# A compact second-stage table, 64-row tiles in the second inverse and a new order, in a two-layer long-convolution and MLP kernel

## The chip, the cores and the metric

The kernel runs on one core of a Trainium2 chip. Its engines are TensorE (PE in the profile; PEld is its weight load), VectorE (DVE), ScalarE (ACT), GpSimd (POOL) and SyncE (SP, which here only issues transfers). Each works through its own list of instructions in order and waits on semaphores for the others. The metric is device time in microseconds; less is better.

## The reference

Two layers follow each other twice, on x with 2048 rows of 512 channels (bfloat16), A being a gated long convolution over the rows and B a multilayer perceptron:

```python
x = A_q
x = x + _A_ref(_layernorm(x), A_k, A_v, A_shift_k, A_ssm_k, A_ssm_D)
x = x + _B_ref(_layernorm(x), B_w1, B_b1, B_w2, B_b2)
x = x + _A_ref(_layernorm(x), A_k, A_v, A_shift_k, A_ssm_k, A_ssm_D)
x = x + _B_ref(_layernorm(x), B_w1, B_b1, B_w2, B_b2)

def _A_ref(q, k, v, shift_k, ssm_k, ssm_D):
    kv = (causal 4-tap filter of k with shift_k) * v        # per channel
    y  = irfft(rfft(kv padded to 4096) * rfft(ssm_k padded to 4096))[:2048]
    return q * (y + kv * ssm_D)

def _B_ref(x, w1, b1, w2, b2):                              # 512 -> 1376 -> 512
    return gelu(_layernorm(x) @ w1 + b1) @ w2 + b2
```

The convolution's result y does not depend on x: it is computed once and serves both layers.

## The kernel before, in words

**The convolution.** The rows are taken in two halves of 1024, and the transform of length 2048 is done by matmuls in steps. For the filter h (`ssm_k`): `ht0` turns the loaded channels by PE transposes (L536), `h1_0` is the first stage (function `stage1`, L553, 128 matmuls of 64 weight columns), and `h2_0` the second stage (`stage2`, L565). A stage-two matmul has a 128x128 weight tile from the table `S2` and a moving operand of 64 columns. `S2` is in fact block-like: for each of the 128 frequencies, its 128 rows are the pairs (part, position, d) with d of 0 to 7, and row d only meets the column of the same d, so seven eighths of the table are zeros. The table of before is stored and loaded with its zeros, 16384 columns in 16 loads of 256 KB (L459). Results of `h2_0` are swapped between even and odd partitions by transfers in SBUF (`swap`, L449) to get real and imaginary parts beside each other.

For the data: `fir0` to `fir3` turn k (L585), run the 4-tap filter as matmuls (L610, 64-row tiles) and multiply by v (L616, VectorE); `x1_0` and `x2_0` are the two stages; products with the filter's transform (L464, VectorE) follow; `i1_0` and `i2_0` are the two steps of the inverse (`inverse1`, L665; `inverse2`, L683). The second half has the same steps with the suffix 1 (`h1_1`, `h2_1`, `p2`, `fir4` to `fir7` by L638 on 32-row tiles, `x1_1`, `x2_1`, `sum`, `i1_1`, `i2_1`). Its `i1_1` needs every product and sum of `x2_1`.

`inverse1` makes eight tiles of two PSUM banks each. For each of eight 128-column groups it adds two matmuls, weights 128x128 from the products p and q, moving operand 128 columns of the table `U`; one eviction of 1024 columns follows for each tile (L469 on ScalarE, L470 on VectorE).

**The layers.** Rows are worked in blocks of 128 to 512: `q` (statistics L797/L798, GpSimd's inverse root L804, a normalization L822 on ScalarE or L823 on VectorE), `y` (times y, add), `z` (the second normalization, then a turn on PE L874 or by a transfer L866), `m1` (L886, four matmuls for each of eleven tiles, Gelu on ScalarE L891) and `m2` (L920, eleven matmuls, added by VectorE L924). The last block's `m2` is cut in column pieces (L909, L913).

**The order.** The program first records all operations (`Prog.op`) with the memory they read and write. Then it takes them in an order written out as a list of numbers, `SEQ`. `ENGS` says for each operation with a choice which engine does it (a ScalarE, v VectorE, p GpSimd), and `BANKS` gives each PSUM tile its first bank. Each engine's list is that order restricted to it; waits are derived from the recorded dependences. Loads and other transfers that SyncE issues are in the same order, so a transfer that waits for data holds all that stand behind it.

```python
for i in range(16):
    tload(t_s2, 128 * 128, i * 1024, R_S2 + i * 1024, 1024)
tload(t_sm, row, 464, R_U, 256)
```

Of the kernel before, what the change touches and what calls it, by code (L numbers as in the profile page):

```python
# [36 lines left out]
class Prog:  # L37
# [62 lines left out]
            "avva")  # L100
    BANKS = ("02220326464004602026041320002442462264542202240064064646402046462667062260046446220462640604660406064226644472"
             "44450442172316353547502206314500451400554567076567013226140174645320543403764701436154766316307007062272260403"
             "71655156407602371631706316706615043246755274432051240747516203416017010")

    def __init__(self, nc):
        self.nc = nc
# [282 lines left out]
def bass_interleave_layers__ssm_conv_h3__mixer_channel_mlp__prompt_kernel(  # L389
# [3 lines left out]
    NS = 352  # L393
# [567 lines left out]
```

## Time and profile before

| | |
|---|---|
| timed runs, median (lowest to highest) | 239.39 us (238.99 to 239.71), 3 runs |
| the profiled execution, first to last instruction | 238.6 us; the profile has no other time for it |
| mean granted clock of TensorE | 0.993 |
| TensorE busy | 226.9 us, 95% |
| VectorE busy | 178.1 us, 75% |
| ScalarE busy | 159.6 us, 67% |
| GpSimd busy | 55.3 us, 23% |
| moved by the transfers | 26.75 MB |

A row of the profile names the engine, the line of the source, the operation, the tiles written and read ("ar" is the one SBUF buffer, "ps" PSUM, "sm" a small float32 buffer) and their shape. Since one helper line records many operations, line 464 stands for all tensor-tensor operations, 469 and 470 for all evictions, and 449 for most transfers. Matmul rows overlap: their own length is latency, and the pace is the distance of starts, which the chain of waits shows. In the chain each row is a start, a length and what ran.

### The profile page before, as it was taken

Reading aid. Unit: us, or ns where it says so; the run is one execution under the profiler, and the core shown is the slowest. Engines: PE = TensorE matmul, PEld = TensorE weight load, DVE = VectorE, ACT = ScalarE, POOL = GpSimd, SP = SyncE. Lnnn points to the kernel's source line nnn. Section 1 sums busy time; section 2 is a strip of 40 time slices with the busy share of each in tenths; the row PEclk is TensorE's granted clock in tenths of the full one; section 3 lists DMA queues with packets and bytes.
Section 4 is the critical chain, followed back from the end, with each engine's and each line's share of the span. In section 5 each row is a group of like instructions: output and inputs, shape, how many; then the busy total and the mean of one; then the engine's idle time right before and its main releaser. Section 6 shows DMA issues by size and latency. Waiting matters only on the chain.

```text
span 238.6 us, 6251 instructions
## 1 busy us (share of the span) xinstructions
PE 226.9 (95%) x2615; PEld 152.3 (64%) x2637; DVE 178.1 (75%) x358; ACT 159.6 (67%) x255; POOL 55.3 (23%) x120
## 2 busy tenths in 40 slices
PE   6998698899999999999999999999999999999995
PEld 3897588885968588667769675644445444444454
DVE  0579869999999999999999999593579469404013
ACT  2586879999996899999768786359036606831630
POOL 2421030104623506446004522303020210200000
PEclk9999979999999999999999999999999999999999
DMA  6999767989946660053100304200300050132202
GB/s 173 350 393 388 272 181 186 257 267 194 163 87 197 153 140 3 1 69 103 54 0 15 80 0 83 49 3 12 78 0 3 18 157 0 25 66 91 84 0 91
DMA packets 41112, 26.75 MB, mean 112 GB/s; under 512 B 23702, under 2 KB 33788, under 8 KB 41084
## 3 DMA queue, kind: packets, MB, share of 16 engines
q1 hardware_dynamic: 40786, 26.20, 40.5%
q8 instruction: 21, 0.34, 0.6%
q10 hardware_dynamic: 298, 0.16, 0.3%
q14 instruction: 7, 0.06, 0.1%
HBM read 15.07 MB, written 2.10 MB: 72 GB/s over the span
## 4 chain that ended last, share of the span: by engine, by line
PE 83%; DVE 6%; DMA 4%; ACT 3%; issue 2%; POOL 1%; SPq 1%; POOLq 0%
PE ps L886 32%; PE ps L920 31%; PE ps L665 6%; PE ps L553 5%; PE ps L565 3%; ACT ar L469 3%; DMA ar<-in_A_ssm_k_dram 2%; DVE ar L464 2%; DMA ar<-ar 2%; DVE ar L616 1%; PE ps L683 1%; PE ps L909 1%; PE ps L638 1%; PE ps L610 1%; DVE ar L470 1%
## 5 line engine op out<-in xcount | busy, mean ns | idle before, releaser
L891 ACT ACTIVATE ar<-ps,sm 128x256 bf16<-128x256 f32 (+4 forms) x143 | 65.4, 525 | 41.0 <-PE ps L886 39.5
L469 ACT ACTIVATE ar<-ps 128x1024 bf16<-128x1024 f32 (+3 forms) x77 | 71.3, 1005 | 16.4 <-PE ps L553 6.4
L886 PE MATMUL ps<-ar 128*128 128x256 bf16 (+4 forms) x568 | 81.5, 297 | 0.3
L920 PE MATMUL ps<-ar 128*128 128x512 bf16 (+1 forms) x324 | 77.2, 379 | 1.1 <-issue 0.3
L886 PEld LDWEIGHTS ps<-ar 128*128 128x128 bf16 (+1 forms) x572 | 52.8, 100 | 28.1 <-ACT ar L891 0.4
L464 DVE TENSOR_TENSOR ar<-ar 128x512 bf16<-128x512 bf16 (+3 forms) x105 | 62.7, 637 | 0.9 <-ACT ar L469 0.4
L920 PEld LDWEIGHTS ps<-ar 128*128 128x128 bf16 (+1 forms) x341 | 32.4, 98 | 33.4 <-ACT ar L891 0.2
L924 DVE TENSOR_TENSOR ar<-ar,ps 128x512 bf16<-128x512 bf16 x31 | 20.7, 678 | 33.2 <-PE ps L920 33.0
L797 DVE BATCH_NORM_STATS2 sm<-ar 128x6 f32<-128x512 bf16 x64 | 42.9, 683 | 0.5
L822 ACT ACTIVATE ar<-ar,sm 128x512 bf16<-128x512 bf16 x34 | 26.4, 811 | 9.5 <-DVE sm L809 8.3
L804 POOL TENSOR_TENSOR sm<-sm 128x2 f32<-128x2 f32 (+2 forms) x26 | 23.6, 909 | 23.8 <-DVE sm L802 22.0
L802 POOL TENSOR_SCALAR sm<-sm 128x2 f32<-128x2 f32 (+2 forms) x21 | 6.4, 304 | 97.3 <-DVE sm L798 97.1
L553 PE MATMUL ps<-ar 128*64 128x128 bf16 x512 | 18.6, 227 | 3.1 <-issue 1.4
L565 PEld LDWEIGHTS ps<-ar 128*128 128x128 bf16 x512 | 18.4, 102 | 3.4 <-ACT ar L469 1.0
L565 PE MATMUL ps<-ar 128*128 128x64 bf16 x512 | 19.6, 199 | 0.5 <-ACT ar L469 0.4
L553 PEld LDWEIGHTS ps<-ar 128*64 128x64 bf16 x512 | 15.7, 114 | 6.1 <-issue 2.6
L812 POOL TENSOR_SCALAR sm<-sm 128x1 f32<-128x1 f32 x43 | 16.1, 390 | 2.0
L470 DVE CAST ar<-ps 128x1024 bf16<-128x1024 f32 x11 | 13.3, 1222 | 4.3 <-PE ps L565 2.8
L665 PE MATMUL ps<-ar 128*128 128x128 bf16 x256 | 15.0, 219 | 0.5 <-DVE ar L464 0.4
L665 PEld LDWEIGHTS ps<-ar 128*128 128x128 bf16 x256 | 14.7, 113 | 1.2 <-DVE ar L464 0.6
L823 DVE TENSOR_SCALAR ar<-ar,sm 128x512 bf16<-128x512 bf16 x30 | 11.8, 410 | 3.4 <-POOL sm L812 3.1
L470 DVE COPY ar<-ps 128x1024 bf16<-128x1024 bf16 (+1 forms) x9 | 5.5, 632 | 8.0 <-PE ps L516 5.3
(41 smaller groups left out, 94.3 us busy)
## 6 DMA issues: line engine op xcount, KB each, us to landing
ar<-tab_s SPq DMA_DIRECT2D x16, 256.0 KB, 9.0
ar<-ar SPq DMA_DIRECT2D x16, 256.0 KB, 3.7
ar<-in_A_ssm_k_dram SPq DMA_DIRECT2D x8, 256.0 KB, 6.8
ar<-in_A_q_dram SPq DMA_DIRECT2D x8, 256.0 KB, 4.7
ar<-in_A_v_dram SPq DMA_DIRECT2D x8, 256.0 KB, 6.1
out_dram<-ar SPq DMA_DIRECT2D x7, 256.0 KB, 2.5
ar<-in_B_w_dram SPq DMA_DIRECT2D x4, 344.0 KB, 4.8
ar<-in_B_w_dram SPq DMA_DIRECT2D x5, 256.0 KB, 4.0
```

The lines of the kernel that those rows point to most:

```text
L464: return P.op(eng, lambda e: e.tensor_tensor(o, a, b, op), dur, reads=[a, b] + list(more), writes=[o])
L469: return e.activation(dst, src(), AF.Copy)
L470: return e.tensor_copy(dst, src())
L553: r = e.matmul(Q(tl, 64 * ri, 64, i * 128, [1, 128]), w, m, start=True, stop=True)
L565: r = e.matmul(Q(tl, 0, 128, i // 8 * 512 + i % 8 * 4, [32, 16], [1, 4]), w, m, start=True, stop=True)
L665: r = e.matmul(Q(tl, 0, 128, i * 128, [1, 128]), w, m, start=n == 0, stop=n == 1)
L797: P.op(DVE, lambda e, sj=sj, x=x: e.bn_stats(sj, x), 600.0, reads=[x], writes=[sj])
L804: P.op(POOL, lambda e: e.tensor_tensor(r, v, hf, ALU.pow), 420.0 + 149.0 * n, reads=[v, hf], writes=[r])
L822: return e.activation(o, x, AF.Identity, bias=u, scale=r)
L886: r = e.matmul(Q(tl, 0, rows, 0, [1, w]), a, m, start=dk == 0, stop=dk == 3)
L891: P.op(ACT, lambda e, dst=dst, tl=tl, rows=rows, bias=bias, w=w: e.activation(dst, Q(tl, 0, rows, 0, [1, w]), AF.Gelu_apprx_tanh, bias=bia ...
L920: r = e.matmul(Q(tl, 0, 128, 0, [1, 512]), ins[fc][0], ins[fc][1], start=fc == 0, stop=fc == 10)
```

## The change

Four things change.

1. The second-stage table is stored without its zeros, 2048 columns, and loaded in two pieces of 256 KB into the place where `w1` goes later (`R_C = R_W1`). Eight columns of 0 and 1 are added to the small table (`sg`), copied once to the float32 buffer (`M_MK`). Sixteen operations tagged `spread` build the dense table: for each half h and each d, the compact half (1024 columns) is multiplied by mask column d, which is 1 in the partitions of that d and 0 elsewhere, and written to 64 runs of 16 columns. Twelve are on VectorE (`tensor_scalar`), four on ScalarE (`activation` with Copy and a scale).
2. The order of the table's columns, and with it of the partitions behind stage two, puts d with the even values first; the table `U` is turned to match.
3. The second half's `inverse1` (`split`) uses 64-row tiles: for each of the 128 former matmuls two with 64 rows of weights, one for the upper and one for the lower 64 partitions, each with 64 moving columns (a strided view of `U`) into its own PSUM bank; 256 matmuls. The first half's stays as it was.
4. `SEQ`, `ENGS` and `BANKS` are new lists. Among other things the loads are reordered: the first are h, q, h, h, h, table, q, table, then four of k and, with one of q among them, four of v (before: h, h, h, four of k, h, q, four of v, h, and the sixteen table pieces among others).

```diff
 class Prog:
-    SEQ = (33, 34, 6, 214, 1, 44, 0,
...
+    SEQ = (
...
     c, s = np.cos(th), np.sin(th)
-    S2 = np.zeros((2, 8, 8, 128, 2, 8, 8))
-    for d in range(8):
-        S2[0, :, d, :, 0, :, d] = c
-        S2[1, :, d, :, 0, :, d] = s
-        S2[0, :, d, :, 1, :, d] = -s
-        S2[1, :, d, :, 1, :, d] = c
-    S2 = S2.transpose(0, 1, 2, 3, 5, 6, 4).reshape(128, 128 * 128)
+    S2 = np.zeros((2, 8, 8, 128, 8, 2))
+    S2[0, :, :, :, :, 0] = c[:, None]
+    S2[1, :, :, :, :, 0] = s[:, None]
+    S2[0, :, :, :, :, 1] = -s[:, None]
+    S2[1, :, :, :, :, 1] = c[:, None]
+    S2 = S2.reshape(128, 2048)
...
-    U = U.transpose(1, 2, 0, 3, 4, 5, 6).reshape(128, 256)
+    U = U[:, :, [0, 2, 4, 6, 1, 3, 5, 7]].transpose(2, 1, 0, 3, 4, 5, 6).reshape(128, 256)
...
+    sg[:, 8:] = np.arange(128)[:, None] % 8 == np.array([0, 2, 4, 6, 1, 3, 5, 7])
...
+    for i in range(2):
+        tload(t_s2, 2048, i * 1024, R_C + i * 1024, 1024)
...
-    for i in range(16):
-        tload(t_s2, 128 * 128, i * 1024, R_S2 + i * 1024, 1024)
+    mk, src = M(0, 128, M_MK, [1, 8]), A(0, 128, R_SG + 8, [1, 8])
+    P.op((DVE, POOL), lambda e, mk=mk, src=src: e.tensor_copy(mk, src), {DVE: 65.0, POOL: 190.0}, reads=[src], writes=[mk])
+    for h in range(2):
+        for d in range(8):
+            o, c, m = A(0, 128, R_S2 + 8192 * h + 16 * d, [128, 64], [1, 16]), A(0, 128, R_C + 1024 * h, [16, 64], [1, 16]), M(0, 128, M_MK + d, [1, 1])
+            def f(e, o=o, c=c, m=m):
+                if e is nc.scalar:
+                    return e.activation(o, c, AF.Copy, scale=m)
+                return e.tensor_scalar(o, c, m, None, ALU.mult)
+            P.op(BOTH, f, {ACT: 912.0, DVE: 340.0}, reads=[c, m], writes=[o])
...
-    def inverse1(p, q, Z):
+    def inverse1(p, q, Z, split):
...
-                    ins.append((i, n, A(0, 128, r + (dg // 4) * 512 + dg % 4, [4, 128]), A(0, 128, R_U + n * 128, [1, 128])))
+                    o = r + (dg // 4) * 512 + dg % 4
+                    if split:
+                        for g in range(2):
+                            ins.append((512 * g + 4 * i, n, A(64 * g, 64, o, [4, 128]), A(64 * g, 64, R_U + n * 128 + g, [8, 16], [2, 4])))
+                    else:
+                        ins.append((i * 128, n, A(0, 128, o, [4, 128]), A(0, 128, R_U + n * 128, [1, 128])))
...
-                    r = e.matmul(Q(tl, 0, 128, i * 128, [1, 128]), w, m, start=n == 0, stop=n == 1)
+                    r = e.matmul(Q(tl, 0, 128, i, *([32, 16], [1, 4]) if split else ([1, 128],)), w, m, start=n == 0, stop=n == 1)
...
+            if split:
+                evac(BOTH, A(0, 128, Z + 64 * j, [1, 2], [512, 16], [2, 32]),
+                     lambda tl=tl: Q(tl, 0, 128, 0, [512, 2], [32, 16], [1, 32]), E1, tl)
+                continue
...
-    inverse1(R_1, R_2, R_3)
+    inverse1(R_1, R_2, R_3, False)
...
-    inverse1(HH, HI, R_Z1)
+    inverse1(HH, HI, R_Z1, True)
```

More of the change, by code (lines that the diff above doesn't have):

```diff
@@ L44 @@
     SEQ = (
[53 rows of a table removed]
-    ENGS = ("apvpvvvpavaavaaaaaavvvaaavvvpvpvaavaaaaavaavvaaaaaaaavavaaaaaavaaavaaaaaappppaaaaaaaaaaaaaaaaaaaaaaaaaaaaapvvp"
-            "paappvppaappvvvpaappaappaappaappaappaappvavpaappvappaappvvppvvvpaappvvavvvvvvavpvvvvppavavpvvvvvpvaaavpvvaaapv"
[L100 to L103, printed above, removed]
[55 rows of a table added]
+    ENGS = (
+            "pvaavvvvvvaavvvvvvpvvvpvpaaaaaavavaaavavaaavvvpvpvvaavaaavaaaaaaaaavaaavavaaaaaaavavaaaaaappvpaaaaaaaaaa"
+            "aaaaaaaaaaaaaaaaaaavpvppvavvvppaapvvvppaavpaappaappaappaappaavpaappaappaapvaappvvppvvvpvappvvaapvavvvvvv"
+            "vvvvvaavavvavvvppavvapvvvavvvvvaa")
+    BANKS = (
+            "06472446040202662604626273640020440464454304006240400264622420266063046260646404042426006424242420460060"
+            "44407446004010202235214533131051432546263377632641205073760160077776106761411420015223703775201233167053"
+            "62330653724071157366300445224175152765572200746657421773405125217406435203517260240")
     def __init__(self, nc):
@@ L439, in bass_interleave_layers__ssm_conv_h3__mixer_channel_mlp__prompt_kernel @@
     R_HRAW1, R_HP1, R_G1, R_HS1, R_K1, R_Z1 = R_W2, R_KT, R_8, R_8, R_1, R_1
+    R_C = R_W1
     R_D, R_W, R_TR = R_W2 + 4096, R_W2 + 4608, R_W2 + 5120
-    M_B1, M_ST, M_MV, M_RS, M_HF, M_NM, M_SG = 0, 16, 208, 240, 256, 260, 276
-    assert M_SG + 1 <= NS
+    M_B1, M_ST, M_MV, M_RS, M_HF, M_NM, M_SG, M_MK = 0, 16, 208, 240, 256, 260, 276, 284
+    assert M_MK + 8 <= NS
     F, S2, U, T2, sg = _tables()
@@ L495, in bass_interleave_layers__ssm_conv_h3__mixer_channel_mlp__prompt_kernel @@
     load_t(A_v, 0, R_8 + 4096, 2)
-    for i in range(16):
-        tload(t_s2, 128 * 128, i * 1024, R_S2 + i * 1024, 1024)
+    P.tag = "spread"
+    mk, src = M(0, 128, M_MK, [1, 8]), A(0, 128, R_SG + 8, [1, 8])
[8 more added lines that the diff above has]
+            P.op(BOTH, f, {ACT: 912.0, DVE: 340.0}, reads=[c, m], writes=[o])
+    P.tag = ""
     tload(t_sm, row, 464, R_U, 256)
@@ L660, in inverse1 @@
                 for n, r in enumerate((p, q)):
-                    ins.append((i, n, A(0, 128, r + (dg // 4) * 512 + dg % 4, [4, 128]), A(0, 128, R_U + n * 128, [1, 128])))
+                    o = r + (dg // 4) * 512 + dg % 4
[4 more added lines that the diff above has]
+                        ins.append((i * 128, n, A(0, 128, o, [4, 128]), A(0, 128, R_U + n * 128, [1, 128])))
             def f(e, ins=ins, tl=tl):
                 for i, n, w, m in ins:
-                    r = e.matmul(Q(tl, 0, 128, i * 128, [1, 128]), w, m, start=n == 0, stop=n == 1)
+                    r = e.matmul(Q(tl, 0, 128, i, *([32, 16], [1, 4]) if split else ([1, 128],)), w, m, start=n == 0, stop=n == 1)
                 return r
-            P.op(PE, f, 16 * 56.0, reads=[x for y in ins for x in y[2:]], tile=tl)
+            P.op(PE, f, 32 * 18.0 if split else 16 * 56.0, reads=[x for y in ins for x in y[2:]], tile=tl)
+            if split:
+                evac(BOTH, A(0, 128, Z + 64 * j, [1, 2], [512, 16], [2, 32]),
+                     lambda tl=tl: Q(tl, 0, 128, 0, [512, 2], [32, 16], [1, 32]), E1, tl)
+                continue
             evac(BOTH, A(0, 128, Z + 64 * j, [512, 16], [8, 8], [1, 8]),
```

108 rows, old and new, of the table SEQ are left out of this document.

## The prediction

> **What bounds the kernel now.** I read the page first, then the same trace cut into stages, the chain of waits in order of time, VectorE's timeline, the groups by shape and SyncE's queue. The page says that TensorE is nearly always busy:
>
> ```profile
> span 238.6 us, 6251 instructions
> PE 226.9 (95%) x2615; PEld 152.3 (64%) x2637; DVE 178.1 (75%) x358; ACT 159.6 (67%) x255; POOL 55.3 (23%) x120
> PE 83%; DVE 6%; DMA 4%; ACT 3%; issue 2%; POOL 1%; SPq 1%; POOLq 0%
> ```
>
> The cut into stages says more. Its columns are busy time of each engine (with instructions), clock, DMA share, GB/s:
>
> ```profile
> core 0: us, PE busy (x) PEld busy (x) DVE busy (x) ACT busy (x) POOL busy (x), PEclk, DMA share, GB/s
> 0.00:20.00 20.00, 17.37 (x301) 13.83 (x301) 9.55 (x14) 9.44 (x10) 5.15 (x18) 1.00 0.91 314
> 20.00:36.00 16.00, 13.07 (x305) 11.73 (x302) 12.77 (x21) 13.22 (x14) 3.35 (x10) 0.89 0.79 263
> 36.00:60.40 24.40, 22.00 (x453) 18.61 (x451) 24.09 (x44) 23.58 (x29) 4.99 (x14) 1.00 0.90 225
> 60.40:124.90 64.50, 63.76 (x904) 48.13 (x914) 63.90 (x112) 56.23 (x112) 23.82 (x40) 1.00 0.40 88
> 124.90:236.20 111.30, 110.71 (x665) 60.03 (x673) 67.53 (x170) 57.08 (x93) 17.98 (x39) 1.00 0.17 43
> ```
>
> From 36 to 124.9 us VectorE (DVE) works 87.99 of 88.9 us, and from 60.4 on TensorE (PE) has no room either. After 124.9 PE alone is full: VectorE is idle 44 us there. Why the border lies there, the chain (start, length, what) and VectorE's timeline show:
>
> ```profile
> 28.20 1.42 issue
> 30.59 3.38 PE ps L565 x64
> 43.91 3.76 PE ps L665 x64
> 51.55 1.03 PE ps L553 x32
> 60.40 3.97 PE ps L886 x68
> 64.37 0.47 PE ps L565 x16
> 72.12 1.05 PE ps L638 x87
> 124.95 0.90 PE ps L665 x16
> 126.49 6.26 PE ps L665 x112
> 236.23 0.29 DVE ar L913
> ```
>
> ```profile
> 5.30 0.20 DVE L470 COPY ar<-ps 128x16 bf16<-128x16 bf16 x1 [5.30 <-PE ps L516]
> 6.30 0.69 DVE L470 COPY ar<-ps 128x1024 bf16<-128x1024 bf16 x1 [0.81 <-PE ps L536]
> 8.62 0.69 DVE L470 COPY ar<-ps 128x1024 bf16<-128x1024 bf16 x1 [1.38 <-PE ps L536]
> 10.46 2.35 DVE L470 CAST ar<-ps 128x1024 bf16<-128x1024 f32 x2 [1.15 <-PE ps L553]
> 17.74 2.36 DVE L616 TENSOR_TENSOR ar<-ps,ar 128x1024 bf16<-128x1024 f32 x2 [1.53 <-PE ps L610]
> 31.43 1.23 DVE L470 CAST ar<-ps 128x1024 bf16<-128x1024 f32 x1 [1.57 <-PE ps L565]
> 40.77 6.70 DVE L464 TENSOR_TENSOR ar<-ar 128x1024 bf16<-128x1024 bf16 x11
> 111.96 12.78 DVE L464 TENSOR_TENSOR ar<-ar 128x2048 bf16<-128x2048 bf16 x14
> ```
>
> The second half's products and sums end at 111.96 + 12.78 = 124.74, less the overlap of pipelined rows; PE's first matmul of the second inverse (L665) starts at 124.95. So the kernel is two pieces: up to X = 124.95 VectorE's work plus VectorE's waits; from X, PE's work, 236.23 - 124.95 = 111.28 us, and 2.37 us of last add and store. The median of the runs, 239.39, stands 0.79 above this span.
>
> **The change, part by part.** The durations come from these groups (busy total, mean ns of one):
>
> ```profile
> L823 DVE TENSOR_SCALAR ar<-ar,sm 128x512 bf16<-128x512 bf16 x30 | 11.8, 410 | 3.4 <-POOL sm L812 3.1
> L754 DVE SCALAR_TENSOR_TENSOR ar<-ar,sm,ps 128x512 bf16<-128x512 bf16 x16 | 11.0, 743 | 0.0
> L647 DVE TENSOR_TENSOR ar<-ps,ar 128x512 bf16<-128x512 f32 x8 | 5.2, 674 | 0.1
> L469 ACT ACTIVATE ar<-ps 128x1024 bf16<-128x1024 f32 x67 | 64.2, 1041 | 10.3 <-PE ps L553 6.4 <-PE ps L665 2.3 <-PE ps L565 1.4
> L822 ACT ACTIVATE ar<-ar,sm 128x512 bf16<-128x512 bf16 x34 | 26.4, 811 | 9.5 <-DVE sm L809 8.3 <-POOL sm L812 1.2
> L470 DVE CAST ar<-ps 128x1024 bf16<-128x1024 f32 x11 | 13.3, 1222 | 4.3 <-PE ps L565 2.8 <-PE ps L553 1.4
> ```
>
> *Inverse on 64-row tiles.* Removed: 128 matmuls of 128 columns, 0.90 + 6.26 = 7.16 us, 56 ns each. Added: 256 of 64 columns, alternating between two row halves and two PSUM banks. The nearest row is L638 (32-row tiles): 1.05 us for 87, 12 ns each. Its 88 matmuls stream 8192 columns, 0.128 ns a column on four tiles; two tiles make that 0.256, or 16.4 ns for 64 columns. I add 1.6 ns for starts: 18 ns, 4.6 us in all. Ends: 12 ns (3.1 us), and no overlap of the halves, which L565's 64-column matmuls price at 0.47 / 16 = 29 ns: 7.5 us, or somewhat more with the stride-2 moving operand that no row shows, say 7.8. Taken: -2.55 us (-4.1 to +0.6). The eight evictions stay on ScalarE; the next inverse waits for the last of them, 8 x 1.0 us (L469) behind X, and in the new order PE has 8.5 us of work ahead of it (its own 4.6 and five groups of L920), so a slower eviction shows at once.
>
> The Trainium skill, page "TensorE: Matmul & The Clock Gate", section "Wait — 56ns, not 53.3ns?", says that start to start never drops below about 25 ns however small the matmul. By that the 256 would take 6.4 us and the kernel 239.2, an estimate from that page. L638's 12 ns in this trace contradict it for alternating row tiles.
>
> *Order behind X.* One group of four and one of three L920 matmuls (0.86 and 0.65 us by 216 ns each) move from before X to behind it: 111.28 - 2.55 + 1.51 = 110.24 us from X to the last matmul.
>
> *Loads.* 14 of 16 table loads go (3.5 MB). They land 9.0 us after issue, and no wait for tab_s is in the chain, so by itself this is worth nothing:
>
> ```profile
> ar<-tab_s SPq DMA_DIRECT2D x16, 256.0 KB, 9.0
> ar<-in_B_w_dram SPq DMA_DIRECT2D x4, 344.0 KB, 4.8
> 52.94 2.60 SPq L766 DMA_TRANSPOSE ar<-in_A_k_dram  x2
> ```
>
> What it buys is the place in front: all four h chunks are among the first five loads (the fourth was eighth), the two compact table pieces sixth and eighth. k and v move back by five places, 5 x 0.83 us at the 314 GB/s of the first stage; behind them queue the four FIR turns on PE, which come after seven h1_0 tiles in the new order, so I cost that at nothing. If those tiles end early, it costs up to 4 us.
>
> *Spread.* New: 12 masked copies on VectorE, 4 on ScalarE, each 128x1024 bf16 from SBUF with one pointer scalar, and a tiny mask copy on GpSimd (0.2 us, its queue has room). Two CASTs in a row take 2.35 us, so 90 of their 1222 ns overlap: 1132 for 1024 elements, against 584 for L647's 512, leaves some 40 ns fixed. A pointer costs 743 - 674 = 70 ns (L754 against L647). L823 has two and takes 410 - 90 = 320: less 140 and 40, 140 ns for 512 elements. That makes 280 + 40 + 70 = 390 ns for 1024 with one pointer. The ends are 0.32 (as L823) and 1.13 (CAST). Taken: 0.40 x 12 = 4.8 us on VectorE. On ScalarE between 1.04 (L469) and 1.62 (twice L822), near the former, 1.1: 4.4 us. ScalarE is idle 13.3 of the first 36 us and covers that; where it doesn't, h2_0 is late by as much.
>
> The Trainium skill, page "VectorE: DVE Perf Modes", section "The perf-mode tier table", gives tensor_scalar on bf16 in SBUF four elements a cycle, which agrees with the 140 ns that L823 leaves. No run here shows an output in runs of 16 elements.
>
> *VectorE ahead of X.* Besides the spread its list up to the last sum changes by two small statistics and evictions more before the first products and about as much less behind them: -0.1 us. So 110.31 us busy become 110.3 + 4.7 = 115.0. Its waits were 124.9 - 110.3 = 14.6, of which 5.30 are the start (kept: its first operation now waits for the second load, and two loads had landed by then) and 9.3 lie mostly between 6 and 36 us, behind PE and ScalarE (0.81, 1.38, 1.15, 1.53, 1.57 above). The spreads and two statistics stand in the list in front of just those waits. What stays is between nothing (X = 120.5) and all (129.8). I keep 3.5: PE's stall at 28.20 (1.42 us) and the 3.38 us for 64 L565 matmuls behind it (53 ns each against 29 later; the clock of this stage is 0.89), which held ScalarE and VectorE at 31.43, came after a thin stretch of PE work that the new order fills; but ScalarE now has 25 activations instead of 21 ahead of h2_0's last eviction, and h2_0's first tile waits for its last spread. X = 115.0 + 5.3 + 3.5 + 0.2 = 124.0.
>
> *PE ahead of X.* The first m1 matmul started at 60.40. In the new order it waits for the last quarter of w1, whose load stands in SyncE's queue behind two k transposes that wait for the last h1_1 matmul: 2.6 us of issue and 4.8 to landing after it. Before, that matmul ended at about 52.6; if the products end as before, 52.4 + 2.6 + 4.8 = 59.8. From m1 to X PE had 64.55 us; two L920 groups leave, one h2_1 tile and four transposes come in (16 x 29 ns, L565's pace, and 0.23): -0.8, so X by PE = 59.8 + 63.75 = 123.6. Both engines meet again; VectorE is last.
>
> Sum: 124.0 + 110.24 + 2.37 = 236.6 us of span, 237.4 with the 0.79.
>
> **The rivals.**
>
> *The spreads are not hidden.* VectorE is the path up to X, and the waits at PE's tiles stay as they were, so all 4.8 us land on it: X = 129.8 at most, 129.8 + 110.24 + 3.16 = 243.2; with three quarters of them left 240.9. It decides from X = 126.0 (239.4): 5.5 us of waits left where I keep 3.5, or spreads of 0.57 us. For it: VectorE's full stretch from 36 us on forgives nothing. Against: its 9.3 us of waits in front.
>
> *The row tiles bring little.* Without any overlap of the two halves 7.5 us instead of 4.6, 240.3; with half of it 238.9. For it: no row has this shape. Against it: L638's 12 ns a matmul, which only tiles side by side give.
>
> *The head shortens as a whole.* Two of VectorE's waits gone altogether, h2_0 earlier without the slow stretch at 30.59, m1 at 58: X = 121.8, 235.2. Against it: the w1 load behind the transposes.
>
> **How the numbers follow.** Chances: forecast (235.8 to 238.6) 0.47; head shortens (234 to 235.8) 0.14; tiles bring little (238.7 to 240.1) 0.11; spreads not hidden (240.1 to 243.2) 0.28. Within 0.3% (238.7 to 240.1) a measurement of this kernel tells no change. Range 234.8 to 241.8: it leaves out the best of the third case and the worst of the slow one.
>
> **What would show it.** Right: the copies at about 0.4 us, i1_1's 256 matmuls in about 4.6 us, VectorE's last product of the first half by 48.5 us (47.4 before), PE's first split matmul near 124.0, and 110 us from there to the last one. Wrong: copies above 0.6 us, a first stage-two matmul (h2_0) later than 25, PE waiting for w1 after 61 us, or waits on ScalarE between the two inverses.

## The result and the profile after

The changed kernel takes 247.39 us (median of 4 runs, 246.74 to 248.00) against 239.55 us for the kernel before (4 runs, 238.99 to 240.07): a ratio of 1.034, with a 95% interval of 1.031 to 1.037. It is 7.8 us slower, where 237.4 was forecast and the range ended at 241.8.

The line numbers of after are shifted: transfers are recorded by L454, table loads by L464, tensor-tensor operations by L469, evictions by L474 (ScalarE) and L475 (VectorE), the masked copies by L512 and L513; stage one is L571, stage two L583, the two steps of the inverse L688 and L710, the stage-two sums of the second half L781, `m1` L913, `m2` L947, the k turns by transfer L793.

The page of after, its first lines, and the same trace cut at the borders of its own stages (X, PE's first split matmul, is now at 129.64):

```profile
span 244.9 us, 6514 instructions
PE 225.3 (92%) x2765; PEld 146.0 (60%) x2765; DVE 183.6 (75%) x378; ACT 165.0 (67%) x259; POOL 49.2 (20%) x108
...
0.00:36.00 36.00, 28.98 (x643) 23.80 (x643) 28.47 (x51) 26.72 (x28) 9.57 (x29) 1.00 0.72 239
36.00:129.64 93.64, 84.98 (x1318) 64.23 (x1315) 85.62 (x151) 79.43 (x140) 22.29 (x46) 1.00 0.42 100
129.64:242.34 112.70, 111.31 (x811) 57.95 (x810) 69.17 (x178) 58.82 (x92) 17.32 (x33) 1.00 0.18 44
```

The kernel before, cut the same way:

```profile
0.00:36.00 36.00, 30.44 (x602) 25.57 (x603) 22.32 (x34) 22.66 (x23) 8.49 (x28) 0.95 0.86 291
36.00:124.95 88.95, 85.81 (x1356) 66.79 (x1365) 88.03 (x155) 79.81 (x140) 28.81 (x53) 1.00 0.54 126
```

The third busy number is VectorE's. Up to 36 us its waits shrank from 13.68 to 7.53 us, as forecast. But from 36 us to X they grew from 0.92 to 8.02 us: the new stretch is 4.7 us longer with 2.4 us less work in it. Behind X the last matmul follows after 112.7 us instead of 111.28. VectorE's timeline of after shows four of its waits behind 26 us, the two largest behind the start of the kernel among them (the bracket is the idle time in front of the row, and who ended it):

```profile
29.49 0.69 DVE L824 BATCH_NORM_STATS2 sm<-ar 128x6 f32<-128x512 bf16 x1 [1.23 <-DMA ar<-in_A_q_dram]
46.33 4.31 DVE L469 TENSOR_TENSOR ar<-ar 128x1024 bf16<-128x1024 bf16 x7 [3.17 <-DMA ar<-ar]
51.81 1.23 DVE L475 CAST ar<-ps 128x1024 bf16<-128x1024 f32 x1 [0.58 <-PE ps L688]
84.15 1.23 DVE L469 TENSOR_TENSOR ar<-ar 128x2048 bf16<-128x2048 bf16 x1 [2.35 <-DMA ar<-ar]
```

The two large ones (3.17 and 2.35 us) wait for `ar<-ar`, the transfers that swap the partitions of a stage-two result. The chain of waits says what held them, and SyncE's timeline what stood in front:

```profile
15.86 9.09 DMA ar<-in_B_b_dram
24.97 0.33 SPq L454
25.34 4.12 DMA ar<-in_A_q_dram
41.62 4.69 DMA ar<-ar
79.66 1.64 SPq L793
81.35 0.60 SPq L454
81.99 3.58 DMA ar<-in_A_v_dram
```

```profile
31.36 6.25 SPq L454 DMA_DIRECT2D ar<-ar  x5
37.66 0.63 SPq L454 DMA_DIRECT2D ar<-in_B_w_dram  x1
38.33 1.33 SPq L454 DMA_DIRECT2D ar<-ar  x2
39.71 0.65 SPq L464 DMA_DIRECT2D ar<-tab_small  x1
40.40 1.17 SPq L454 DMA_DIRECT2D ar<-in_B_w_dram  x2
41.62 1.54 SPq L454 DMA_DIRECT2D ar<-ar  x1
```

In after's order the eighth swap (operation 95) stands behind two `w2` loads that wait until PE has turned the second filter half, out of whose place they write; `U` (operation 35) stands behind the other seven swaps and lands when PE has waited 1.74 us for it; the second `b1` load waits 9 us for the first, with q behind it; a k turn and a v load stand between the second half's swaps. That SyncE's queue was the cause was then a theory (Q below). Its rivals: the masked copies lie on VectorE's path (S), and the split's gain is lost at its eviction (E), since behind X the rows read:

```profile
129.64 1.78 PE L688 MATMUL ps<-ar 64*128 64x64 bf16 x96
131.80 0.72 PE L688 MATMUL ps<-ar 64*128 64x64 bf16 x32 [0.38 <-ACT ar L474]
135.32 1.95 PE L688 MATMUL ps<-ar 64*128 64x64 bf16 x96 [0.53 <-ACT ar L474]
140.06 0.60 PE L710 MATMUL ps<-ar 128*128 128x512 bf16 x2 [0.30 <-ACT ar L474]
130.40 9.61 ACT L474 ACTIVATE ar<-ps 128x1024 bf16<-128x1024 f32 x8 [1.91 <-PE ps L688]
```

Eight evictions take 9.61 us, 1.2 us each, where before seven took 6.52 us, 0.93 each; PE waits 1.21 us for them.

The last stretch up to X does not run on VectorE alone. From 98 us on the chain of waits is mostly on ScalarE, then on the transfer that turns a block of `z`, then on PE. Four of its rows (a start, a length and what ran):

```profile
98.36 1.52 ACT ar L849 x2
101.69 3.77 ACT ar L474 x4
117.35 2.99 DMA ar<-ar
120.39 6.29 PE ps L913 x56
```

PE comes from there to X at 129.64 without a wait, and VectorE's last sum has ended 0.44 us before.

### The profile page after: what moved, and what is told of

Read it like the earlier page. It is cut to its first block, busy times and chain, and to the rows that moved or that the text cites. A ratio compares the mean times of both kernels' runs of the same rounds, so it can differ in the third digit from the quotient of the medians.

```text
span 244.9 us, 6514 instructions
## 1 busy us (share of the span) xinstructions
PE 225.3 (92%) x2765; PEld 146.0 (60%) x2765; DVE 183.6 (75%) x378; ACT 165.0 (67%) x259; POOL 49.2 (20%) x108
## 4 chain that ended last, share of the span: by engine, by line
PE 43%; DVE 16%; DMA 13%; ACT 11%; issue 6%; SPq 5%; POOL 4%; POOLq 0%; DVEq 0%
PE ps L913 21%; PE ps L947 17%; ACT ar L474 9%; DVE ar L469 5%; DMA ar<-ar 4%; DMA ar<-in_B_b_dram 4%; DVE ar L475 4%; DMA ar<-in_A_q_dram 3%; SPq L454 3%; DVE sm L824 2%; SPq L893 2%; DVE ar L951 2%; ACT ar L918 2%; PE ps L710 1%; DMA ar<-in_A_v_dram 1%
## 5 line engine op out<-in xcount | busy, mean ns | idle before, releaser
L913 PE MATMUL ps<-ar 128*128 128x256 bf16 (+5 forms) x572 | 82.6, 297 | 2.0 <-DMA ar<-ar 1.2
L474 ACT ACTIVATE ar<-ps 128x1024 bf16<-128x1024 f32 (+3 forms) x77 | 73.3, 1041 | 15.0 <-PE ps L571 8.1
L947 PE MATMUL ps<-ar 128*128 128x512 bf16 (+1 forms) x341 | 79.6, 379 | 0.0
L913 PEld LDWEIGHTS ps<-ar 128*128 128x128 bf16 (+1 forms) x572 | 52.0, 100 | 31.0 <-DMA ar<-ar 2.4
L469 DVE TENSOR_TENSOR ar<-ar 128x512 bf16<-128x512 bf16 (+3 forms) x105 | 63.3, 638 | 6.0 <-DMA ar<-ar 5.5
L947 PEld LDWEIGHTS ps<-ar 128*128 128x128 bf16 (+1 forms) x341 | 32.6, 98 | 34.6
L831 POOL TENSOR_TENSOR sm<-sm 128x2 f32<-128x2 f32 (+2 forms) x26 | 22.0, 845 | 59.4 <-DVE sm L829 57.9
L571 PE MATMUL ps<-ar 128*64 128x128 bf16 x512 | 17.7, 221 | 6.3 <-DVE ar L475 2.9
L571 PEld LDWEIGHTS ps<-ar 128*64 128x64 bf16 x512 | 14.9, 110 | 9.1 <-DVE ar L475 3.7
L583 PE MATMUL ps<-ar 128*128 128x64 bf16 x512 | 18.3, 193 | 1.3 <-ACT ar L474 1.0
L583 PEld LDWEIGHTS ps<-ar 128*128 128x128 bf16 x512 | 16.8, 98 | 4.1 <-ACT ar L474 2.4
L688 PE MATMUL ps<-ar 64*128 64x64 bf16 (+1 forms) x384 | 13.1, 203 | 4.4 <-DMA ar<-tab_small 1.7
L688 PEld LDWEIGHTS ps<-ar 64*128 64x128 bf16 (+1 forms) x384 | 12.0, 114 | 6.1 <-ACT ar L474 3.3
L475 DVE CAST ar<-ps 128x1024 bf16<-128x1024 f32 x12 | 14.4, 1216 | 0.8 <-PE ps L688 0.6
L839 POOL TENSOR_SCALAR sm<-sm 128x1 f32<-128x1 f32 x35 | 11.8, 351 | 1.7
L825 DVE BATCH_NORM_AGGREGATE sm<-sm 128x2 f32<-128x6 f32 x64 | 10.9, 175 | 0.8
```

The source lines that it names most:

```text
L469: return P.op(eng, lambda e: e.tensor_tensor(o, a, b, op), dur, reads=[a, b] + list(more), writes=[o])
L474: return e.activation(dst, src(), AF.Copy)
L475: return e.tensor_copy(dst, src())
L571: r = e.matmul(Q(tl, 64 * ri, 64, i * 128, [1, 128]), w, m, start=True, stop=True)
L583: r = e.matmul(Q(tl, 0, 128, i // 8 * 512 + i % 8 * 4, [32, 16], [1, 4]), w, m, start=True, stop=True)
L688: r = e.matmul(Q(tl, 0, 128, i, *([32, 16], [1, 4]) if split else ([1, 128],)), w, m, start=n == 0, stop=n == 1)
```

## The experiments

Unless it says otherwise, a kernel is the changed one with the edit shown. Times are medians; "before" was timed beside each set and lay between 238.7 and 239.6 us. The sets ran on different chips, so a difference between two of them carries that of their "before" as well; the ratio to "before" is given where that matters.

**Two transfers forward.** They are `U` (operation 35) and the last swap of the first half (95).

```diff
     SEQ = (
...
-        131, 93,
+        131, 35, 93,
...
-        178, 94, 193, 188, 35,
+        178, 94, 95, 193, 188,
...
-        150, 95, 147,
+        150, 147,
```

> The changed kernel (247.39 us) with two transfers moved forward in SyncE's queue and nothing else: the seventh-issued swap of the first half's stage-two result ahead of the two w2 loads that wait for the second filter half's transposes, and the 64 KB of U ahead of the first swap. Theory Q (the time went into transfers that stand in SyncE's queue behind something that waits): VectorE's 3.17 us wait at 43.15 for that swap falls under 1 us and PE's 1.74 us wait at 44.26 for the table goes; the first m1 matmul starts at 60 to 61 instead of 62.64, and the time is 244.4 to 245.4. Theory S (the spread's copies on VectorE and ScalarE are the loss): both engines keep their work, the wait turns into another one at the same place, and the time stays at 246.5 to 248.

Measured: 244.53 us (243.78 to 245.44; 1.023 of before, 1.018 to 1.028). VectorE's wait at that place:

```profile
44.12 4.30 DVE L469 TENSOR_TENSOR ar<-ar 128x1024 bf16<-128x1024 bf16 x7 [1.32 <-DMA ar<-ar]
```

It fell from 3.17 to 1.32 us, the first `m1` matmul started at 60.28 instead of 62.64, and X came at 127.04. Two lines of the order are worth 2.9 us. Theory Q holds for this place; 1.32 us are left of a wait that it put under 1.

**The bias later, the last v load earlier.**

```diff
     SEQ = (
...
-        64, 213, 33,
+        64, 33,
...
-        77, 214, 128,
+        77, 128,
...
-        215, 208, 133, 480, 124, 121, 84, 216, 125,
+        208, 213, 133, 480, 124, 121, 84, 125,
...
-        207, 152,
+        207, 214, 215, 216, 152,
```

> The changed kernel with only the two loads of b1 (the second waits for the first to land) and their two GpSimd copies moved behind the loads of q, w1 and w2 that stood behind them. Theory Q: the third q load is issued at about 16 us instead of 25.34, VectorE's 1.23 us wait at 29.49 goes, and at most that much of the time, 246.0 to 247.2, since the wait for the swap at 43 comes later and takes it up. Theory S: no change, 247.4.

```diff
     SEQ = (
...
-        462, 290, 421,
+        462, 290, 293, 286, 421,
...
-        570, 286, 515,
+        570, 515,
...
-        512, 293, 267,
+        512, 267,
```

> The changed kernel with only the last k transpose and the last v load of the second half moved in SyncE's queue, from between the second half's swaps to ahead of the z2 transposes. Theory Q: VectorE's 2.35 us wait at 84.15 for the swaps shrinks by the 2.3 us of issue that stood between them, to under 0.5, and the time falls by 1.5 to 2.3, to 245.1 to 245.9. Rival: ScalarE's activations are as late from 98 us on and set X anyway; then the wait goes but the time stays above 246.7.

Measured: 247.51 us (245.65 to 248.91) and 247.39 us (246.63 to 249.12), no gain in either. The wait for q was gone in the first, and the wait for the second half's swaps fell from 2.35 to 1.01 us in the second. What took the gain is in PE's timeline, the first row of the bias kernel, the second of the v kernel:

```profile
50.75 5.39 PE L688 MATMUL ps<-ar 128*128 128x128 bf16 x64 [2.77 <-DVE ar L469]
```

```profile
31.71 1.70 PE L571 MATMUL ps<-ar 128*64 128x128 bf16 x32 [1.49 <-DVE ar L475]
```

After a wait, 64 matmuls took 5.39 us (84 ns each) and 32 took 1.70 us (53 ns). The granted clock was 0.68 over the first stretch, with 0.50 from 52 to 55 us, and 0.58 over the second. In after the same 64 took 3.76 us behind a wait of 1.68 us, at a clock of 1.00. The granted clock of all runs of these two kernels was 0.986 to 0.993, that of three of after's four runs 1.0.

The slow stretch of the v kernel lies at 31.7 us, and its edit only acts from some 77 us on, so the edit did not make it. Its rival, that ScalarE sets X anyway, would fit the time as well. The traces speak against it: in the kernels of the new order X follows 45.5 to 46.1 us behind the start of the product that waits for the second half's swaps (in after 84.15 and 129.64, in the first experiment 81.33 and 127.04), so a wait that ends earlier moves X. In the v kernel it did not end earlier (84.11 against 84.15), because the slow stretch had put off the data of the swaps. So neither run prices its move cleanly; only the sum does:

**All three moves.**

> All three moves together, no arithmetic touched. Theory Q: the waits of 3.17, 1.23 and 2.35 us go, in sum 6.8 us less what turns into other waits; X (the first split matmul) at 123.5 to 125.5 instead of 129.64, time 241 to 243.5. Theory S: X stays above 128, time above 245.5.

Measured: 243.32 us (242.04 to 243.57; 1.017 of before, 1.012 to 1.021), X at 126.46 where theory Q had 123.5 to 125.5, clock 1.0. Of VectorE's 8.02 us of waits between 36 us and X, 5.42 are left. Without touching any arithmetic the order of SyncE's queue gave back 4.1 us of the 7.8; the time lies within theory Q's range (up to 243.5), but what remained it did not forecast.

**The copies, twice and half.** On top of the three moves:

```diff
+            o2 = A(0, 128, (R_5, R_6)[h] + 16 * d, [128, 64], [1, 16])
...
-                if e is nc.scalar:
-                    return e.activation(o, c, AF.Copy, scale=m)
-                return e.tensor_scalar(o, c, m, None, ALU.mult)
+                for x in (o2, o):
+                    if e is nc.scalar:
+                        r = e.activation(x, c, AF.Copy, scale=m)
+                    else:
+                        r = e.tensor_scalar(x, c, m, None, ALU.mult)
+                return r
...
```

> The changed kernel with all three queue moves (243.32 us) and each of the sixteen masked copies executed twice, the second time into a part of SBUF that is not yet in use: 12 x 0.39 = 4.7 us more on VectorE and 4 x 1.05 = 4.2 us more on ScalarE in the first 30 us. Theory Q (the copies fill time in which VectorE waited anyway, the loss is in the queue): under 1.5 us more, 243.3 to 244.8. Theory S (the copies lie on the path to X): 246 to 248, and then the copies as they are cost the changed kernel some 3 to 5 us as well.

The half kernel leaves out the second half of the table (its eight copies shrink to 16 columns), and every stage-two matmul uses the first:

```diff
+            if h:
+                o, c = A(0, 128, R_S2 + 8192 + 16 * d, [1, 16]), A(0, 128, R_C + 1024, [1, 16])
+                f.__defaults__ = (o, c, m)
             P.op(BOTH, f, {ACT: 912.0, DVE: 340.0}, reads=[c, m], writes=[o])
...
-        ins = [(i, A(0, 128, R_S2 + (16 * t + i) * 128, [1, 128]), A(0, 128, G + (16 * t + i) * 8, [1024, 8], [1, 8])) for i in range(16)]
+        ins = [(i, A(0, 128, R_S2 + (16 * (t % 4) + i) * 128, [1, 128]), A(0, 128, G + (16 * t + i) * 8, [1024, 8], [1, 8])) for i in range(16)]
```

> The changed kernel with all three queue moves (243.32 us), where the masked copies of the table's second half write 16 columns only and the stage-two products take the first half's table for all their tiles: left out is the second half of the table, so the values are those of a wrong table; instructions and waits are the same. 6 x 0.39 = 2.3 us less on VectorE, less some 0.1 us for each of the six small copies, and 2 x 1.05 us less on ScalarE. If the copies lie fully on the path to X: 241.3 to 241.9. If there are waits that would come back in their place: 242.5 to 243.3.

Measured: twice 247.32 us (4.0 more), half 242.74 us (0.6 less). The two don't give one price. Twice puts 4.2 us more work on VectorE up to X (118.82 instead of 114.60), and X comes 4.0 us later, at 130.45: in the kernel with the three moves VectorE waits only 0.54 us between 8.67 and 36 us, so work added there lands on the path nearly whole. Half takes 1.7 us of VectorE's work off (112.91). In its profiled execution X came 1.42 us earlier, at 125.04, but that was the fastest of its five (241.85), and the medians differ by 0.6 us alone. So between a third and most of what was taken off came back as time, and what the copies already there cost in this order stays open. Theory S's forecast of the first run came true, and its conclusion, that these copies cost 3 to 5 us, did not follow from it.

**The split alone, in the order of before.** Its dense table is kept, with the columns of S2 and U turned as in the change.

```diff
-    inverse1(HH, HI, R_Z1)
+    inverse1(HH, HI, R_Z1, True)
```

> The kernel before, in its own order and with its sixteen dense table loads (their columns permuted as the split needs them), with only the second half's inverse split into 64-row tiles. Theory E (the split's own gain is taken back by its eviction, which writes with stride 2: 1.20 us each start to start in the changed kernel against 0.93 before): the 256 matmuls take about 5.0 us instead of 7.2, the eight evictions end 1.3 + 8 x 1.2 = 10.9 us behind X where PE has 7.2 us of work, so PE waits about 3 us there and the time is 239.4 to 240.4. Rival P (as predicted: the split is worth its 2.55 us): 236.8 to 237.6.

Measured: 240.44 us (1.004 of before, 1.001 to 1.007). The second step of PE's inverse (L694 here) began 10.6 us behind X instead of 9.5, after 2.7 us of waits for ScalarE's evictions. X, the last two waits, and the evictions:

```profile
123.54 0.72 PE L672 MATMUL ps<-ar 64*128 64x64 bf16 x32
132.10 1.67 PE L931 MATMUL ps<-ar 128*128 128x512 bf16 x7 [0.70 <-ACT ar L471]
134.18 1.04 PE L694 MATMUL ps<-ar 128*128 128x512 bf16 x4 [0.41 <-ACT ar L471]
124.30 9.83 ACT L471 ACTIVATE ar<-ps 128x1024 bf16<-128x1024 f32 x8 [0.96 <-PE ps L672]
```

Theory E holds: with this eviction the split gains nothing. The first attempt to relieve it was to give four of the eight evictions to VectorE, here (`ENGS` and `SEQ`, the statistics of block q9 go behind the last eviction, 371) and in the same way on top of the queue moves:

```diff
-aaaaaaaaaaaaaaa
+aaaaaaavavaaavv
...
-        722, 682, 732, 368, 863, 804, 367, 805, 864, 865, 866, 364, 806,
-        369, 360, 767, 809, 365, 810, 361,
+        722, 682, 732, 368, 804, 367, 805, 364, 369, 806,
+        360, 767, 809, 365, 810, 361,
...
```

> The same as the split alone, but four of its eight evictions on VectorE, taken in turn with ScalarE, and the q9 statistics that stood between them behind them. Theory E: the evictions end some 6 to 7.5 us behind X, PE's wait for them falls under 0.7 us, and the time is 236.8 to 238.3, faster than the kernel before by 1 to 2.5 us. Rival P: as the split alone, 236.8 to 237.6 for both. If the split's matmuls had no gain of their own: 239.4 for both.

> The changed kernel with all three queue moves (243.32 us) and four of the split's eight evictions on VectorE. Theory E: PE's waits for ScalarE behind X, 1.2 us together (0.38, 0.53, 0.30), go; 241.8 to 242.5. If the evictions do not set the pace there: 243.3.

Measured: 244.74 and 247.01 us, 4.3 and 3.7 us slower than without the edit. VectorE's queue is not free just behind X: it works through statistics of which the next blocks are in need. In the first kernel an eviction stood behind them until 129.37 and PE waited for it; in the second the normalizations that now stood behind evictions were late, and PE waited for the `z` turns:

```profile
130.69 1.90 PE L672 MATMUL ps<-ar 64*128 64x64 bf16 x64 [3.87 <-DVE ar L472]
```

```profile
142.78 2.74 PE L913 MATMUL ps<-ar 128*128 128x256 bf16 x12 [2.76 <-DMA ar<-ar]
```

**The eviction in another element order.** The evictions stay on ScalarE.

```diff
-                evac(BOTH, A(0, 128, Z + 64 * j, [1, 2], [512, 16], [2, 32]),
-                     lambda tl=tl: Q(tl, 0, 128, 0, [512, 2], [32, 16], [1, 32]), E1, tl)
+                evac(BOTH, A(0, 128, Z + 64 * j, [512, 16], [2, 32], [1, 2]),
+                     lambda tl=tl: Q(tl, 0, 128, 0, [32, 16], [1, 32], [512, 2]), E1, tl)
```

> The split alone in the order of the kernel before (240.44 us), with the evictions written in runs of 64 neighbours and read from the two PSUM banks in turn. Theory E: the eight evictions take 7.5 to 8 us instead of 9.8, PE's waits there fall from 2.7 to some 0.7 us, and the time is 237.8 to 238.8, under the kernel before. If the alternating read costs as much as the stride-2 write: 240.4 again.

> The changed kernel with all three queue moves (243.32 us), where the split inverse's evictions go through the same elements in another order: written in runs of 64 neighbours, read from the two PSUM banks in turn. If the stride-2 write makes them slow (Theory E): 0.93 to 1.0 us each instead of 1.20, PE's waits behind X (1.2 us) mostly go, 242.0 to 242.6. If the alternating read costs as much: 243.3 or more.

Measured: the split alone with it 238.33 us (12 runs; 0.996 of before, 0.994 to 0.999), 2.1 less than with the stride-2 write; the three queue moves with it 241.41 us, 1.9 less. ScalarE's row of the first kernel, and of the second with PE's rows beside it:

```profile
127.00 6.52 ACT L471 ACTIVATE ar<-ps 128x1024 bf16<-128x1024 f32 x7 [0.39 <-PE ps L672]
```

```profile
126.62 3.78 ACT L474 ACTIVATE ar<-ps 128x1024 bf16<-128x1024 f32 x4 [1.91 <-PE ps L688]
125.86 2.56 PE L688 MATMUL ps<-ar 64*128 64x64 bf16 x128
128.58 1.46 PE L947 MATMUL ps<-ar 128*128 128x512 bf16 x6 [0.16 <-issue]
```

The evictions are back at 0.93 us, though they now read PSUM from two banks in turn, and in the second kernel PE's waits for them are down to two of about 0.25 us, each before the last 32 matmuls of 128. The stride of the write was the whole excess: the evictions of stage two, which read PSUM in an order like that of the slow form and write runs of 32 neighbours, take 0.92 us each as well (18 evictions of ScalarE, those among them, in 16.64 us in the kernel of the old order below). The split alone with this eviction is faster than both the kernel before and the changed one.

**Without the split,** on top of the queue moves:

```diff
-    inverse1(HH, HI, R_Z1, True)
+    inverse1(HH, HI, R_Z1, False)
```

> The changed kernel with all three queue moves (243.32 us) and the second half's inverse on the full array again, as in the kernel before. Theory E: the split's own saving there is 2.1 us on PE less 1.2 us of waits for its evictions, so without it 243.8 to 244.6. If the split is worth its full 2.55 us: 245.9. If it is worth nothing in this order: 243.3.

Measured: 243.77 us. The split as the change has it is worth 0.45 us (243.77 - 243.32), or 0.7 by the ratios to "before" (1.020 and 1.017); with the other eviction it is worth 2.4 us (243.77 - 241.41).

**The copies in the old order, the dense loads in the new.** With the queue moves and the better eviction the changed kernel was still 2.1 us above before. Two kernels should tell whether the copies or the order hold them. The first has the order, engines and banks of before, into which the compact loads (operations 4 and 5), the mask copy (18) and the copies of the first half (19 to 26) and of the second (27 to 34) are set. It has the numbers of the changed kernel; part of its order is:

```diff
+        36, 37, 8, 217, 1, 47, 0, 38, 39, 6, 9, 2, 42, 18, 54, 3, 41, 13, 4, 55, 10, 5, 44, 11, 12, 48, 7, 198, 17, 14,
+        57, 49, 15, 56, 16, 70, 136, 58, 19, 22, 50, 68, 71, 45, 137, 59, 60, 61, 62, 69, 72, 74, 51, 63, 102, 73, 106,
+        75, 52, 46, 103, 43, 53, 100, 101, 104, 391, 111, 108, 105, 64, 66, 107, 23, 24, 25, 26, 65, 115, 118, 40, 109,
+        119, 110, 134, 392, 393, 116, 67, 20, 21, 132, 112, 130, 199, 135, 113, 27, 142, 433, 434, 30, 133, 28, 140,
...
```

> The order, engines and banks of the kernel before, with the compact table loads (sixth and eighth in SyncE's queue), the mask copy and the sixteen masked copies set into waits of VectorE (12) and ScalarE (4) as its profile shows them, and the split with contiguous evictions; beside split_contiguous (238.33 us), which has the dense loads. If the copies are the cost: their 4.7 us on VectorE less the waits that they fill, 241 to 243. If the order is: the copies fit into VectorE's 9 us of waits ahead of 36 us and the time is 237.5 to 239.3.

The second has a dense table again, as before the change, loaded behind the last v load. The copies are gone, and two tiny operations on the mask stand in their place:

```diff
-        tload(t_s2, 2048, i * 1024, R_C + i * 1024, 1024)
+        tload(t_s2, 128 * 128, i * 1024, R_S2 + i * 1024, 1024)
...
+    for i in range(2, 16):
+        tload(t_s2, 128 * 128, i * 1024, R_S2 + i * 1024, 1024)
...
```

> The new order with the queue moves and the contiguous evictions (queue_contiguous, 241.41 us), but the table loaded dense: sixteen 256 KB loads behind the last of h, k and v, no copies on VectorE and ScalarE. If the copies are the cost: VectorE's list is 4.7 us shorter ahead of X and the time 237 to 239. If the order is: VectorE waits for stage-two tiles and swaps instead, 240.4 to 242.4; if the loads come too late in the new order, PE waits for tab_s at the first stage-two tile and it is above 242.4.

Measured: 238.52 us in the old order (0.997 of before, 0.995 to 0.999), as with dense loads there (238.33). In that order the copies cost nothing that can be told. The dense loads in the new order gave 252.23 us, which tells little of the copies: the second filter half, which the new order turns earlier, now queued behind them.

```profile
30.65 1.07 PE L550 MATMUL ps<-ar 128*128 128x128 bf16 x8 [9.86 <-DMA ar<-in_A_ssm_k_dram]
```

The same parts in the two orders, first the new (241.41 us), then the old (238.52 us), each to its own X:

```profile
0.00:36.00 36.00, 29.92 (x662) 24.68 (x663) 29.57 (x52) 27.92 (x30) 9.19 (x27) 1.00 0.76 250
36.00:125.86 89.86, 83.27 (x1285) 63.60 (x1296) 84.85 (x150) 78.26 (x138) 23.13 (x48) 1.00 0.43 100
```

```profile
0.00:36.00 36.00, 30.97 (x659) 25.92 (x659) 28.05 (x48) 27.76 (x29) 9.15 (x29) 1.00 0.60 199
36.00:123.08 87.08, 83.68 (x1294) 64.46 (x1303) 86.28 (x153) 78.08 (x138) 30.00 (x53) 1.00 0.55 124
```

VectorE's work up to X is the same, 114.42 and 114.33 us. The new order does 1.5 us more of it ahead of 36 us and then waits 5.01 us up to X, the old one 0.80. In the difference of X, 2.78 us, lies the 2.9 us difference of the times. Of the 5.01 us, 2.7 stand at swaps:

```profile
38.57 3.70 DVE L469 TENSOR_TENSOR ar<-ar 128x1024 bf16<-128x1024 bf16 x6 [0.30 <-DMA ar<-ar]
43.47 4.30 DVE L469 TENSOR_TENSOR ar<-ar 128x1024 bf16<-128x1024 bf16 x7 [1.21 <-DMA ar<-ar]
79.99 1.22 DVE L469 TENSOR_TENSOR ar<-ar 128x2048 bf16<-128x2048 bf16 x1 [1.17 <-DMA ar<-ar]
```

**Stage-two tiles first.** In the new order the first swap is issued at 31.4 us, in the old at 27.65, since two stage-one tiles of x come ahead of two of the four tiles that it needs. On top of the queue moves and the better eviction:

```diff
-        479, 132, 135, 129, 202, 120, 208, 213, 133, 480, 124, 121, 84, 125, 78,
-        529, 79, 481, 86, 85, 87, 82, 585, 122, 83,
+        479, 78, 135, 129, 202, 82, 208, 213, 79, 480, 124, 83, 84, 125, 132,
+        529, 133, 481, 86, 85, 87, 120, 585, 122, 121,
```

(78 and 82 are the stage-two tiles, 79 and 83 their evictions; 132 and 120 are the stage-one tiles of x. Besides, eviction 83 goes to VectorE and 121 to ScalarE, and the tiles of 82 and 120 exchange their banks.)

> The new order with the queue moves and the contiguous evictions (queue_contiguous, 241.41 us), and two stage-two tiles of the first filter half exchanged with two stage-one tiles of the first x half, so that all four tiles that the first two swaps wait for come ahead of the others. If these late swaps hold VectorE: the first swap is issued at about 29 us instead of 31.4, VectorE's waits for swaps of 0.30 and 1.21 us at 38.6 and 43.5 go, and the time is 239.7 to 240.5. If the second group of swaps, whose tiles stay where they are, sets the wait: within 0.5 of 241.41.

Measured: 240.91 us, 0.5 less in the medians, but 1.011 of the before timed beside it where the other was 1.010: no gain that can be told. The first swap was issued at 29.17, and the wait at the last one stayed:

```profile
43.14 4.30 DVE L469 TENSOR_TENSOR ar<-ar 128x1024 bf16<-128x1024 bf16 x7 [1.19 <-DMA ar<-ar]
```

So the second group of swaps sets it. The 2.9 us are located (VectorE's waits between 36 us and X, more than half of them at swaps), but what in the new order, its engines and its banks makes them was not taken apart further, and neither was what the copies cost there.

## Why the prediction was wrong

The loss in three steps, each the difference of two medians: SyncE's queue 4.1 us (247.39 to 243.32), the stride of the split's eviction 1.9 (to 241.41), the rest of the new order, with its engines and banks, 2.9 (to 238.52). By the ratios to "before" the three are 4.2, 1.6 and 3.1 us. With the three taken out, the change's own parts are a little faster than the kernel before.

- **What bounds the kernel** (VectorE to X, then PE) was right up to some 94 us and behind X. In between, the chain of after runs over ScalarE, a turn by transfer and PE, and VectorE's last sum ends 0.44 us before X. VectorE's work to X, forecast at 115.0 us, was 114.10. **The copies** were right: 0.40 us forecast on VectorE and 1.1 on ScalarE; four start 0.39 us apart, and the groups say 472 and 1153 ns with latency:

```profile
L513 DVE TENSOR_SCALAR ar<-ar,sm 128x1024 bf16<-128x1024 bf16 x12 | 5.3, 472 | 0.0
L512 ACT ACTIVATE ar<-ar,sm 128x1024 bf16<-128x1024 bf16 x4 | 4.6, 1153 | 0.0
```

- **VectorE ahead of X is the step that failed.** "I keep 3.5" of its waits took the stretch behind 36 us as full, since it was full in the order before. It treated a wait as something that a stage has; it is something that an order has. Of the 15.5 us of waits up to X, 4.84 are the start; 2.7 more lie ahead of 36 us, near the forecast; 8.02 lie behind it, where I had none, 5.52 of them (3.17 and 2.35) in two waits for swaps. X came at 129.64 instead of 124.0.
- **Loads, "worth nothing by themselves" and k and v "at nothing".** That held for h, k and v, but I followed SyncE's queue only to `w1`. What is not in that paragraph is each transfer that SyncE issues in a new place: a swap behind `w2` loads that wait for PE, `U` behind swaps, q behind `b1`, v and a k turn between swaps. A list of SyncE's entries, written from the new order alone with what each waits for, would have shown it.
- **PE ahead of X**, 59.8 for the first `m1`: it was 62.64, because the products ended at 50.6 and not by 48.5, by the swap's wait. With the swap's wait down to 1.32 us the first `m1` came at 60.28. The wait that I had named there (`w1` behind two k turns) did not come last.
- **The inverse on 64-row tiles**, 18 ns a matmul, was right: in after's row of 96 the starts are 16.7 ns apart ((1.78 - 0.19) / 95, with 0.19 us as the last one's own length). In the kernel with the better eviction, 128 of them take 2.56 us (125.86 to 128.42) with one wait of 0.25 us among them, so 5.1 us for 256 instead of 4.6; without the split they take twice 3.74 us. The saving is 2.3 us on PE and 2.4 in the times, where 2.55 was forecast. L638's 12 ns, from which the price was worked out, had the last one's length in it too: its starts are 10.8 ns apart. I had weighed the Trainium skill's page "TensorE: Matmul & The Clock Gate", section "Wait — 56ns, not 53.3ns?", by which starts are never under 25 ns apart (6.4 us); the trace disagrees for tiles taken in turn (16.7 ns). The term that failed there is the eviction, "8 x 1.0 us": 1.2 us each. I had even noted that a slower one shows at once, and had priced the form by rows that all write neighbours.
- **Order behind X**, 110.24 us to the last matmul: 112.7 in after. The moved groups were right: without the split it was 112.97 (126.15 to 239.12), and 111.28 + 1.51 = 112.79 were forecast. So the 2.5 us too many lie in the split's saving, 0.3 us there with the slow evictions. With the better eviction it was 111.1 (125.86 to 236.96), a saving of 1.9.
- **The rivals.** The time lies above all of them. "The spreads are not hidden" comes nearest (up to 243.2) and is wrong in its mechanism: it kept the waits ahead of 36 us, and these shrank from 13.68 to 7.53 us. In the old order the copies cost 0.2 us, less than can be told; in the new one their price stays open. "The row tiles bring little" was wrong on the matmuls and right on the sum, by the eviction, which it didn't name. No rival was the order itself or SyncE's queue.
- **The base.** I added 0.79 us to the span. In the runs here a time lies 1.8 us above its span (246.74 and 244.9 in the profiled execution of after). In the profiled execution of before the 64 stage-two matmuls at 30.59 took 53 ns each, at a granted clock of 0.52, and the split alone, the same up to X, reached it at 123.54 instead of 124.95. Both errors nearly cancel.

## What to carry to other kernels

A transfer queue that works in order is an engine like the others: when an order changes, write down for each entry of it what it waits for and what stands behind, swaps and small tables too, before a wait is called hidden. A wait that a profile doesn't show in a stretch is a property of that order, and an engine that was full there may be waiting in the next one with the same work. Price an eviction by its write pattern. In the one shape measured here, where the element order was free, it paid to write neighbours and to put the jumps on the read side.

## What was not expected of the hardware

- ScalarE's eviction of 128x1024 from PSUM took 0.93 us with neighbours written and 1.20 to 1.23 us with every second bfloat16 written; reading two PSUM banks element by element in turn cost nothing. The Trainium skill, page "SBUF — State Buffer", section "Door 1: The DMA port swizzle (why `[64,N]` ≈ `[32,N]`)", says that strides of up to 8 bfloat16 are free; for this write they were not.
- PE was slower for some microseconds behind some of its waits: 5.39 us instead of 3.76 for 64 matmuls behind 2.77 us of waiting (granted clock 0.68), 1.70 us instead of 1.08 for 32 behind 1.49 us (0.58), but the usual 3.76 us behind 1.68 us in after (1.00). The Trainium skill, page "TensorE: Matmul & The Clock Gate", section "Part 1: The HAM clock gate (the "warmup" mystery)", puts the fall at an idle window of about 3.4 us; here shorter waits, in a stretch with several, were enough, and not each of them was.
